# Top k of attention scores on pairs: the threshold from two sorted lists instead of one

## The chip, the cores and the metric

The kernel runs on one core of a Trainium2 chip. The time is the device time of one execution, in microseconds (us). TensorE (PE) does the matrix products, VectorE (DVE) the top-k search, ScalarE (ACT) copies, exponentials and activations, GpSimd (POOL) the masking, and SyncE (SP) issues the DMAs. Each engine works off its own queue in the order in which the program gives it work, and engines wait for one another through semaphores.

## The reference: what is computed

Attention that keeps only the 32 largest scores of each row, and behind it a two-layer perceptron:

```python
q, k, v: (8 batches, 8 heads, 576 positions, 64)  float32
scores = q @ k.T / sqrt(64)                       # 576 scores in a row
kth    = 32nd largest score of each row
scores = where(scores >= kth, scores, -1e9)
attn   = softmax(scores)
x      = (attn @ v), heads side by side           # (4608, 512)
h      = x @ w_in                                 # w_in  (512, 2048), float64
out    = max(0.01 * h, h) @ w_out                 # w_out (2048, 512), float64
```

A row's threshold `kth` is all that the top-k search has to deliver, with the row's maximum, which the softmax subtracts.

## The kernel before

**Units.** Heads are taken in pairs (32 pairs over the batches). A `Unit` is 128 query rows of both heads of a pair, or the 64 left-over rows of both heads of two pairs: 256 rows of scores in either case, held as two halves i = 0 and 1 of 128 partitions each. There are 144 units. A unit's scores lie in `u.both`, 128 partitions by 2 halves by 576 float32; `u.s[i]` is one half.

**One unit's way through the engines.** `scores` (L168): PE multiplies into PSUM, ACT copies to `s_sb` (L184). `top_k` (L186): DVE alone. It works in four rounds. In a round, an eight-largest instruction (`nc.vector.max`, MAX8 in the trace, L193) takes the eight largest of a half's 576 scores, for each half; then, in all rounds but the last, `match_replace` (MATCH_VALUE_LOAD and MATCH_REPLACE8 in the trace, L196) writes a copy in which these eight are overwritten by the lowest float. So each half has 4 MAX8 and 3 replacements, all 576 long; the 32nd largest is the last value of the fourth round. `mask` (L201): POOL computes `nbias` from the maximum (L205), then for each half `pen` = (score < threshold) * a large negative number (L207) and adds it to the scores (L209). `exponents`, `sums` and `normalize` run on ACT; `reciprocals` (L219) is one small DVE instruction in between (L221). `transpose` (L226) splits the floats into 16-bit halves on ACT (L233) and turns them with DMAs; `weigh_values` (L250) multiplies by v on PE. The perceptron (`mlp`, L269) works on chunks of up to 256 tokens on PE and ACT.

**The order of the work.** The schedule is written out by hand: a loop over steps (L392), one unit per step entering `top_k`, with the earlier units at later stages. In step s the top-k search is on unit s (`cur`), the mask on unit s-1 (`old`), the exponentials, the reciprocal, the normalization and the transposition on unit s-2 (`older`). `top_k` is a generator; each call of `slot(n)` (n = 0 to 3) runs it to its next `yield`, that is one round. Between the slots the loop puts perceptron matmuls (`mlp_steps`) on PE, by a budget that spreads the work at hand over the steps. The reciprocal stands behind `slot(2)`, so on DVE it lies in front of the last round. The scores of the next units are made ahead (`s_sb` has five buffers). Before the first unit, the weights are converted from float64 bits to float32 (`convert_weights`, L100 to L124), mostly on DVE.

The functions that the diff touches, with the line numbers of the profile:

Of the kernel before, what the change touches and what calls it, by code (L numbers as in the profile page):

```python
# [7 lines left out]
F32 = mybir.dt.float32  # L8
U32 = mybir.dt.uint32
U16 = mybir.dt.uint16  # L10
AF = mybir.ActivationFunctionType
ALU = mybir.AluOpType

NKC = 5

# [2 lines left out]
def kernel(  # L18
# [13 lines left out]
    nc = tc.nc  # L32
    NPAIR, P, S = qT.shape
    D = P // 2
    DFF, DMODEL = moe_w_out.shape[0], moe_w_in.shape[0]
    TOPK = 32
    SLOPE = 0.01
    LOWEST = -3.4028234663852886e38
    SCALE = float(D) ** -0.5
    MASKED = -1e9 / SCALE  # L40
    HP = DMODEL // P
    B = NPAIR // HP
    HS = S // 2
    NFC = DFF // P
    ROUNDS = TOPK // 8
    WCH = 1024
    LEFT = S % P
    assert D == 64 and S == 576 and HP == 4 and B % 2 == 0 and LEFT == 64
# [5 lines left out]
    const = ctx.enter_context(tc.tile_pool(name="const", bufs=1))  # L54
# [3 lines left out]
    work = ctx.enter_context(tc.tile_pool(name="work", bufs=2))  # L58
    small = ctx.enter_context(tc.tile_pool(name="small", bufs=5))
# [6 lines left out]
    range_lo, range_hi = ends[:, 0:1], ends[:, 1:2]  # L66
    nc.vector.memset(range_lo, -896.0)
    nc.vector.memset(range_hi, 255.0)

    w_in = [const.tile([P, DFF], F32, name=f"w_in{c}") for c in range(HP)]  # L70
    w_out = [const.tile([P, 4, DMODEL], F32, name=f"w_out{c}") for c in range(NFC // 4)]
# [28 lines left out]
    def convert_weights(dst, raw, on_vector):  # L100
# [6 lines left out]
        exf = ex.bitcast(F32)  # L107
        nc.vector.tensor_scalar(ex, hi, 20, 0x7FF, ALU.logical_shift_right, ALU.bitwise_and)  # L108
        nc.vector.tensor_scalar(man, hi, 0xFFFFF, None, ALU.bitwise_and)

        if on_vector:
            nc.vector.tensor_scalar(ex, ex, 1151.0, 896.0, ALU.min, ALU.max)
            nc.scalar.activation(ex, ex, AF.Copy, bias=-896.0 * 2.0 ** 23, scale=2.0 ** 23)
        else:
# [5 lines left out]
        nc.vector.scalar_tensor_tensor(out=dst, in0=man, scalar=2.0 ** -20, in1=frac,  # L120
                                       op0=ALU.mult, op1=ALU.add)
        nc.vector.scalar_tensor_tensor(out=ex, in0=hi, scalar=0x80000000, in1=ex,  # L122
                                       op0=ALU.bitwise_and, op1=ALU.bitwise_or)
        nc.vector.tensor_tensor(dst, dst, exf, ALU.mult)  # L124

# [59 lines left out]

    def top_k(u):  # L186

        u.tops = small.tile([P, 2, ROUNDS, 8], F32, name="tops")
        rest = [work.tile([P, S], F32, name=f"rest{i}", bufs=1) for i in range(2)]
        src = u.s  # L190
        for r in range(ROUNDS):
            for i in range(2):
                nc.vector.max(out=u.tops[:, i, r, :], in_=src[i])  # L193
            if r + 1 < ROUNDS:
                for i in range(2):
                    nc.vector.match_replace(out=rest[i], in_to_replace=u.tops[:, i, r, :],  # L196
                                            in_values=src[i], imm_value=LOWEST)
                src = rest
            yield

    def mask(u, i):  # L201
        if i == 0:
            u.nbias = small.tile([P, 2], F32, name="nbias")
            u.z = small.tile([P, 2], F32, name="z")
            nc.gpsimd.tensor_scalar(u.nbias, u.tops[:, :, 0, 0], -SCALE, None, ALU.mult)  # L205
        pen = work.tile([P, S], F32, name="pen", bufs=1)
        nc.gpsimd.tensor_scalar(pen, u.s[i], u.tops[:, i, ROUNDS - 1, 7:8], MASKED,  # L207
                                ALU.is_lt, ALU.mult)
        nc.gpsimd.tensor_tensor(u.s[i], u.s[i], pen, ALU.add)  # L209

    def exponents(u, i):
# [30 lines left out]
    def x_at(token):  # L242

        c = 0
        while token >= CHUNKS[c]:
            token -= CHUNKS[c]
            c += 1
        return c, token
# [89 lines left out]
    for n, u in enumerate(steps):  # L338
        if u is None:
            continue  # L340
        ch, _ = x_at(u.b * S + u.q0)
# [39 lines left out]
    with tc.manual_schedule():  # L381
# [10 lines left out]
        for s in range(len(steps) + LAG + 1):  # L392
            cur, old = unit(s), unit(s - 1)
            older, oldest, new = unit(s - 2), unit(s - LAG), ()
            if s % 2 == 0:
                new = [u for u in steps[s + 2:s + 4] if u]
            picks = top_k(cur) if cur else iter(())
            budget = slot_budget(s)

# [6 lines left out]
            if old:  # L406
                mask(old, 0)
                mask(old, 1)
# [91 lines left out]
```

## Time and profile before

| | |
|---|---|
| median of 3 runs | 1600.31 us (1598.17 to 1601.62) |
| profiled execution: time / span | 1596.01 us / 1594.1 us |
| mean granted TensorE clock | 0.988 |
| busy PE | 1396.0 us (88%) |
| busy DVE | 1480.3 us (93%) |
| busy ACT | 1115.8 us (70%) |
| busy POOL | 1078.6 us (68%) |
| DVE MAX8 (L193) | 608.2 us for 864 and 202.1 us for 288 instructions |
| DVE replacement (L196) | 423.6 us for 576 and 211.8 us for 288 instructions |
| POOL `pen` (L207) / add (L209) | 638.4 us / 406.5 us, 288 instructions each |

The profile is of one execution; its span is what lies between the first and the last instruction in it, its time some 2 us more. "Busy" is the time in which an engine had an instruction in it. Neighbouring instructions of DVE overlap by their ends: the mean length of one is longer than the distance from its start to the next one's start.

### The profile page before, as it was taken

How to read it: one execution, taken by the hardware profiler on the slowest of the kernel's cores; microseconds unless marked ns; L12 is line 12 of the kernel's file. 1: busy time of each engine (PE TensorE's matmuls, PEld its weight loads, DVE VectorE, ACT ScalarE, POOL GpSimd, SP SyncE). 2: the span in 40 equal slices, each digit the busy share in tenths (PEclk: the TensorE clock that was granted, in tenths of full speed). 3: DMA queues.
4: the chain of work that ended last, by engine and by line, in shares of the span. 5: the costliest groups of instructions: out<-in, count | busy, mean ns of one | idle time of the engine just before them, and what ended most of it. 6: DMA issues, size and time to landing. Idle time of an engine off the chain costs nothing.

```text
span 1594.1 us, 23761 instructions
## 1 busy us (share of the span) xinstructions
PE 1396.0 (88%) x8064; PEld 931.4 (58%) x8064; DVE 1480.3 (93%) x3114; ACT 1115.8 (70%) x2133; POOL 1078.6 (68%) x724
## 2 busy tenths in 40 slices
PE   0024977999999999999999999999999999999998
PEld 0013654757575757575757575757575756666664
DVE  8999989999999999999999999999999999999700
ACT  5626766778787877677877777777777777777720
POOL 0037767777777777777777777777777777777700
PEclk9998989999999999999999999999999999999999
DMA  6714436554655446544655456645655455545420
GB/s 226 268 42 119 120 112 184 146 147 126 185 142 149 133 127 184 161 114 131 192 142 144 132 133 173 169 127 136 184 150 148 121 161 135 157 121 141 128 68 14
DMA packets 400313, 227.00 MB, mean 142 GB/s; under 512 B 343360, under 2 KB 343360, under 8 KB 399168
## 3 DMA queue, kind: packets, MB, share of 16 engines
q1 hardware_dynamic: 400192, 225.49, 49.7%
q8 instruction: 63, 1.03, 0.3%
q14 instruction: 58, 0.48, 0.1%
HBM read 46.14 MB, written 94.37 MB: 88 GB/s over the span
## 4 chain that ended last, share of the span: by engine, by line
DVE 67%; PE 22%; ACT 6%; DMA 4%; issue 1%; SPq 0%; ACTq 0%
DVE tops L193 34%; DVE rest L196 28%; PE ph L277 10%; PE pz L289 6%; PE psc L175 3%; PE po L257 3%; ACT split L233 2%; DMA wT<-apart 2%; ACT s_sb L224 1%; DVE ex L122 1%; ACT s_sb L212 1%; DVE w_in L124 1%; DVE ex L108 1%; DVE w_in L120 1%; DMA apart<-split 1%
## 5 line engine op out<-in xcount | busy, mean ns | idle before, releaser
L207 POOL TENSOR_SCALAR pen<-s_sb,tops 128x576 f32<-128x576 f32 x288 | 638.4, 2216 | 304.6 <-DVE tops L193 272.2
L193 DVE MAX8 tops<-rest 128x8 f32<-128x576 f32 x864 | 608.2, 746 | 0.0
L277 PE MATMUL ph<-x,w_in 128*128 128x256 f32 (+1 forms) x2432 | 526.1, 373 | 40.7 <-ACT gT L283 40.7
L277 PEld LDWEIGHTS ph<-x,w_in 128*128 128x128 f32 x2432 | 440.1, 192 | 132.5 <-ACT gT L283 57.8
L289 PE MATMUL pz<-w_out,gT 128*128 128x512 f32 x1152 | 509.1, 597 | 3.4 <-ACT gT L283 3.4
L196 DVE MATCH_REPLACE8 rest<-tops,rest 128x576 f32<-128x576 f32 x576 | 423.6, 743 | 0.0
L209 POOL TENSOR_TENSOR s_sb<-s_sb,pen 128x576 f32<-128x576 f32 x288 | 406.5, 1412 | 24.0
L289 PEld LDWEIGHTS pz<-w_out,gT 128*128 128x128 f32 x1152 | 216.6, 191 | 269.2 <-issue 263.4
L224 ACT ACTIVATE s_sb<-s_sb,rz 128x576 f32<-128x576 f32 x288 | 207.3, 767 | 225.1 <-DVE rz L221 223.5
L233 ACT COPY split<-s_sb 128x1152 uint16<-128x1152 uint16 x288 | 318.0, 1154 | 2.3
L175 PE MATMUL psc<-kt,qt 64*128 64x288 f32 (+1 forms) x1280 | 201.2, 448 | 109.3 <-ACT s_sb L184 79.8
L212 ACT ACTIVATE s_sb<-s_sb,nbias 128x576 f32<-128x576 f32 x288 | 220.7, 773 | 15.4 <-POOL s_sb L209 15.4
L257 PE MATMUL po<-wT,vt 128*64 128x128 f32 (+1 forms) x3200 | 184.8, 270 | 40.1 <-DMA wT<-apart 38.8
L175 PEld LDWEIGHTS psc<-kt,qt 64*128 64x128 f32 (+1 forms) x1280 | 112.1, 185 | 180.7 <-ACT s_sb L184 86.6
L196 DVE MATCH_REPLACE8 rest<-tops,s_sb 128x576 f32<-128x576 f32 x288 | 211.8, 743 | 0.0
L257 PEld LDWEIGHTS po<-wT,vt 128*64 128x64 f32 x3200 | 162.7, 140 | 74.9 <-issue 40.1
L193 DVE MAX8 tops<-s_sb 128x8 f32<-128x576 f32 x288 | 202.1, 744 | 0.0
L283 ACT ACTIVATE gT<-ph 128x256 f32<-128x256 f32 (+1 forms) x304 | 109.5, 373 | 126.9 <-PE ph L277 124.7
L184 ACT COPY s_sb<-psc 128x576 f32<-128x576 f32 x288 | 169.9, 646 | 19.5 <-PE psc L175 19.2
L205 POOL TENSOR_SCALAR nbias<-tops 128x2 f32<-128x2 f32 x144 | 33.5, 233 | 105.2 <-DVE tops L193 92.4
L212 ACT ACTIVATION_READ_ACCUMULATOR s_sb<-s_sb,nbias 128x1 f32 x288 | 56.3, 195 | 0.0
L221 DVE RECIPROCAL rz<-ze 128x2 f32<-128x2 f32 x144 | 22.7, 157 | 30.6 <-ACT ze L217 30.4
(26 smaller groups left out, 292.9 us busy)
## 6 DMA issues: line engine op xcount, KB each, us to landing
apart<-split SPq DMA_DIRECT2D x288, 288.0 KB, 2.1
vt<-in_vk_dram SPq DMA_DIRECT2D x32, 320.0 KB, 3.4
qt<-in_qT_dram SPq DMA_DIRECT2D x32, 288.0 KB, 3.9
kt<-in_kT_dram SPq DMA_DIRECT2D x32, 288.0 KB, 4.5
out_dram<-o_sb SPq DMA_DIRECT2D x36, 256.0 KB, 2.6
raw<-in_moe_w_in_dram SPq DMA_DIRECT2D x8, 1024.0 KB, 5.1
raw<-in_moe_w_out_dram SPq DMA_DIRECT2D x8, 1024.0 KB, 4.9
wT<-apart SPq DMA_TRANSPOSE x144, 4.5
```

The source lines that it names most:

```text
L175: nc.tensor.matmul(ps[i][r0:r0 + u.rows, half, 0:HS], qt[d, u.q0:u.q0 + u.rows], kt[d, half * HS:(half + 1) * HS], start=True, stop=True,)
L184: nc.scalar.copy(u.s[i].rearrange("p (h n) -> p h n", h=2), ps[i][:, :, 0:HS])
L193: nc.vector.max(out=u.tops[:, i, r, :], in_=src[i])
L196: nc.vector.match_replace(out=rest[i], in_to_replace=u.tops[:, i, r, :], in_values=src[i], imm_value=LOWEST)
L207: nc.gpsimd.tensor_scalar(pen, u.s[i], u.tops[:, i, ROUNDS - 1, 7:8], MASKED, ALU.is_lt, ALU.mult)
L209: nc.gpsimd.tensor_tensor(u.s[i], u.s[i], pen, ALU.add)
L212: nc.scalar.activation(u.s[i], u.s[i], AF.Exp, bias=u.nbias[:, i:i + 1], scale=SCALE, accum_out=u.z[:, i:i + 1])
L224: nc.scalar.activation(u.s[i], u.s[i], AF.Copy, bias=0.0, scale=u.rz[:, i:i + 1])
L233: nc.scalar.copy(split, pairs[:, :, h])
L257: nc.tensor.matmul(po[side * D:(side + 1) * D, o, :], vt[:, c, side, :], u.wT[:, c + side * NKC if c + 1 < NKC else c, r:r + n], start=(c ...
L277: nc.tensor.matmul(ph[:, 0:n], w_in[c][:, f * P:(f + 1) * P], x[c][:, 0:n], start=(c == 0), stop=(c == HP - 1),)
L289: nc.tensor.matmul(pz[0:m, 0:DMODEL], gT[f][:, r0:r0 + m], w_out[f // 4][:, f % 4, :], start=(f == 0), stop=(f == NFC - 1),)
```

## The change

`top_k` no longer works on the 576 scores of a half, but on 288 pairs: score n of the first 288 with score n of the last 288. Two elementwise instructions over both halves (128 x 2 x 288) make `greater` (the larger of each pair) and `less` (the smaller). The search then takes the 16 largest of `less` (2 rounds) and the 32 largest of `greater` (4 rounds), each on 288 elements per half, with the replacement done in place. Of the 32 largest of all, at most 16 can be smaller ones of their pair, since the larger one stands before each. The 32nd of all is then the largest, over j = 0 to 16, of the lesser of two values: the j-th of the `less` list (plus infinity's stand-in for j = 0, kept in column 7 of the constant tile `lesser`) and the (32 - j)-th of the `greater` list. That is one elementwise minimum on 2 x 17 elements (`bounds`) and one reduction by maximum (`kth`).

The work per unit goes to the slots in another way: slot 0 now has the two elementwise instructions, the whole search of `less` and the first round of `greater`; slots 1 and 2 have a round of `greater` each, and slot 3 the last one, `bounds` and `kth`. The mask reads `u.kth` in place of the last value of the list.

```diff
+AX = mybir.AxisListType
...
-    ROUNDS = TOPK // 8
...
+    lesser = const.tile([P, 2, 8 + TOPK // 2], F32, name="lesser")
+    nc.vector.memset(lesser[:, :, 7:8], -LOWEST)
...
     def top_k(u):
 
-        u.tops = small.tile([P, 2, ROUNDS, 8], F32, name="tops")
-        rest = [work.tile([P, S], F32, name=f"rest{i}", bufs=1) for i in range(2)]
-        src = u.s
-        for r in range(ROUNDS):
-            for i in range(2):
-                nc.vector.max(out=u.tops[:, i, r, :], in_=src[i])
-            if r + 1 < ROUNDS:
+        u.tops = small.tile([P, 2, TOPK], F32, name="tops")
+        u.kth = small.tile([P, 2], F32, name="kth")
+        pairs = [work.tile([P, 2, HS], F32, name=name, bufs=1) for name in ("greater", "less")]
+        for of, op in zip(pairs, (ALU.max, ALU.min)):
+            nc.vector.tensor_tensor(of, u.both[:, :, 0:HS], u.both[:, :, HS:S], op)
+
+        def largest(of, n, to):
+            for r in range(n):
                 for i in range(2):
-                    nc.vector.match_replace(out=rest[i], in_to_replace=u.tops[:, i, r, :],
-                                            in_values=src[i], imm_value=LOWEST)
-                src = rest
-            yield
+                    nc.vector.max(out=to[:, i, 8 * r:8 * r + 8], in_=of[:, i, :])
+                if r + 1 < n:
+                    for i in range(2):
+                        nc.vector.match_replace(
+                            out=of[:, i, :], in_to_replace=to[:, i, 8 * r:8 * r + 8],
+                            in_values=of[:, i, :], imm_value=LOWEST)
+                    yield
+
+        for _ in largest(pairs[1], TOPK // 16, lesser[:, :, 8:]):
+            pass
+        yield from largest(pairs[0], TOPK // 8, u.tops)
+
+        bounds = small.tile([P, 2, TOPK // 2 + 1], F32, name="bounds", bufs=1)
+        nc.vector.tensor_tensor(bounds, u.tops[:, :, TOPK - 1:TOPK // 2 - 2:-1],
+                                lesser[:, :, 7:], ALU.min)
+        nc.vector.tensor_reduce(out=u.kth, in_=bounds, axis=AX.X, op=ALU.max)
+        yield
...
-            nc.gpsimd.tensor_scalar(u.nbias, u.tops[:, :, 0, 0], -SCALE, None, ALU.mult)
+            nc.gpsimd.tensor_scalar(u.nbias, u.tops[:, :, 0], -SCALE, None, ALU.mult)
...
-        nc.gpsimd.tensor_scalar(pen, u.s[i], u.tops[:, i, ROUNDS - 1, 7:8], MASKED,
-                                ALU.is_lt, ALU.mult)
+        nc.gpsimd.tensor_scalar(pen, u.s[i], u.kth[:, i:i + 1], MASKED, ALU.is_lt, ALU.mult)
```

Queue by queue, the other engines' instructions are the same in number and order; only what `pen` waits for is another instruction of DVE.

## The prediction

> **What bounds the kernel now.** First the page's busy shares, its slices and the chain that ended last.
>
> ```profile
> PE 1396.0 (88%) x8064; PEld 931.4 (58%) x8064; DVE 1480.3 (93%) x3114; ACT 1115.8 (70%) x2133; POOL 1078.6 (68%) x724
> ...
> DVE  8999989999999999999999999999999999999700
> ...
> DVE 67%; PE 22%; ACT 6%; DMA 4%; issue 1%; SPq 0%; ACTq 0%
> ```
>
> VectorE is full from the first slices to slice 38 (about 1506 us), and it carries two thirds of the chain. What follows is a tail of some 88 us of transposition and perceptron that the change doesn't touch. PE looks full too, but the busy table by stretches of 100 us has DVE at 100% in most of them, so DVE sets the pace. The question is the length of one unit on DVE. The timeline of DVE shows it (start, length, both in us):
>
> ```profile
> 801.57 1.41 DVE L193 MAX8 tops<-s_sb 128x8 f32<-128x576 f32 x2
> 802.89 0.08 DVE L196 MATCH_VALUE_LOAD rest<-tops,s_sb 128x8 f32 x1
> 802.95 0.75 DVE L196 MATCH_REPLACE8 rest<-tops,s_sb 128x576 f32<-128x576 f32 x1
> 803.61 0.09 DVE L196 MATCH_VALUE_LOAD rest<-tops,s_sb 128x8 f32 x1
> 803.68 0.75 DVE L196 MATCH_REPLACE8 rest<-tops,s_sb 128x576 f32<-128x576 f32 x1
> 804.34 1.42 DVE L193 MAX8 tops<-rest 128x8 f32<-128x576 f32 x2
> ...
> 809.88 0.16 DVE L221 RECIPROCAL rz<-ze 128x2 f32<-128x2 f32 x1
> 809.96 1.40 DVE L193 MAX8 tops<-rest 128x8 f32<-128x576 f32 x2
> 811.27 1.41 DVE L193 MAX8 tops<-s_sb 128x8 f32<-128x576 f32 x2
> ```
>
> The starts count, not the lengths, since neighbours overlap: an instruction lasts 0.746 but the next starts 0.66 later. A unit takes 811.27 - 801.57 = 9.70: four pairs of MAX8 (1.32, 1.33, 1.33, 1.31 from start to next start), three pairs of replacements (804.34 - 802.89 = 1.45) and the reciprocal (0.08). 144 units are 1397 us of the span. The waits of DVE in that stretch are small:
>
> ```profile
> DVE rz L221 <- ACT ze L217: 30.4, 14, 10.6
> ```
>
> 4.2 and 10.6 of these 30.4 us lie in the tail, 15.6 us among the units.
>
> Two more views price what is new. The timeline of the weight conversion has two-input elementwise instructions, and a dependence on the instruction directly before:
>
> ```profile
> 15.25 1.22 DVE L120 SCALAR_TENSOR_TENSOR w_in<-w_in,raw 128x1024 f32<-128x1024 uint32 x1
> 16.39 1.22 DVE L122 SCALAR_TENSOR_TENSOR ex<-raw,ex 128x1024 uint32<-128x1024 uint32 x1
> 17.64 1.23 DVE L124 TENSOR_TENSOR w_in<-w_in,ex 128x1024 f32<-128x1024 f32 x1
> ```
>
> L122 doesn't need L120's result and starts 1.14 after it; L124 needs L122's and starts 1.25 after it. So waiting for one's direct predecessor costs 0.11. Lastly, POOL's timeline in the same unit:
>
> ```profile
> 810.89 2.22 POOL L207 TENSOR_SCALAR pen<-s_sb,tops 128x576 f32<-128x576 f32 x1 [1.85 <-DVE tops L193]
> 813.20 1.42 POOL L209 TENSOR_TENSOR s_sb<-s_sb,pen 128x576 f32<-128x576 f32 x1
> 814.71 2.21 POOL L207 TENSOR_SCALAR pen<-s_sb,tops 128x576 f32<-128x576 f32 x1
> 817.01 1.41 POOL L209 TENSOR_TENSOR s_sb<-s_sb,pen 128x576 f32<-128x576 f32 x1
> 818.51 0.23 POOL L205 TENSOR_SCALAR nbias<-tops 128x2 f32<-128x2 f32 x1
> 820.59 2.22 POOL L207 TENSOR_SCALAR pen<-s_sb,tops 128x576 f32<-128x576 f32 x1 [1.85 <-DVE tops L193]
> ```
>
> `pen` starts 0.18 after the MAX8 that it waits for has ended (809.96 + 0.75 = 810.71). POOL works 7.85 of the 9.70 and is idle for 1.85.
>
> **The change on DVE, without other engines.** Fixed part and elements first, from start to start: MATCH_VALUE_LOAD takes 0.065 for 8 elements, MAX8 0.66 for 576, L120's form 1.14 for 1024. The slopes are (0.66 - 0.065) / 568 = 1.05 ns per element and (1.14 - 0.66) / 448 = 1.07. I take 1.05: an instruction of 288 is 0.30 shorter than one of 576, and the fixed parts are 0.055 for MAX8 and 0.065 for the two-input form. Removed per unit: 8 MAX8 and 6 replacements at 576. Added:
> - 6 pairs of MAX8 at 1.32 - 0.60 = 0.72: 4.34 (with the same spread of a hundredth by position).
> - 4 pairs of replacements at 1.45 - 0.60 = 0.85: 3.39.
> - `greater` and `less`, 576 elements each: 0.605 + 0.065 = 0.67, twice: 1.34. The first MAX8 on `less` needs the instruction directly before it: 0.11.
> - The last MAX8 is the direct predecessor of `bounds`: 0.11. `bounds`, 34 elements: 0.035 + 0.065, and `kth` waits for it: 0.11, together 0.21. `kth` to the next instruction: 0.10 (bounds: the reciprocal's 0.08 below, 0.2 above if reducing two short rows has a longer start; I take the value near the reciprocal's row, which is as small).
> - The reciprocal stays: 0.08.
>
> Sum: 4.34 + 3.39 + 1.34 + 0.11 + 0.11 + 0.21 + 0.10 + 0.08 = 9.68 against 9.70. The searched elements fall from 14 x 576 to 20 x 288, 2304 fewer or 2.4 us; six more fixed parts (0.06 for each of 4 MAX8, 0.12 with the value load for each of 2 replacements: 0.5), two passes over the data (1.34) and three waits (0.33) and the ending (0.2) eat all of it. By this sum alone the kernel gains 0.02 per unit, 144 x 0.02 = 3 us. An error of 0.1 per unit in the unmeasured parts would be 14 us either way.
>
> **What is moved.** POOL's `pen` now waits for `kth`, behind both last MAX8 and the two endings, not for the first of the two last MAX8; that is some 0.8 later in a unit, but it is later in each unit alike, so it costs that once, in the tail. The exponentials that follow run a step later (ACT waited for POOL's result 15.4 us in all, in two places). Behind the new waits on DVE only the top-k itself is queued. The reciprocal stands 0.8 from the unit's end as a MAX8 pair, `bounds` and `kth`, against 1.31 before: about half a microsecond later for ACT's normalization, which waited for it 223.5 us in all without being the bound, and as much more slack for `ze`. No DMA and no PE instruction moves.
>
> **What it collides with.** MAX8 and replacements read one tensor and keep 0.746 and 0.743 whatever POOL does beside them. `greater` and `less` read two, and no row of before has such an instruction beside a busy POOL: in the conversion POOL is idle. They come at a bad place. `kth` ends about 0.09 after `greater` has started, so by the 0.18 above `pen` starts some 0.27 after the start of `greater`, in all 143 units that follow another. Bounds for the cost on DVE: nothing (POOL waits, within its 1.85 of idle time), or one whole `pen`, 2.2, if `less` is held until `pen` ends. Nothing below zero: POOL gives DVE no time. Between them: both share reads element by element. A `pen` has a start of about 0.2 (the 2-element `nbias` takes 0.23), then 576 reads in 2.0, 3.5 ns each. From 0.47 to the end of `less` (1.35, less the tail gaps) some 0.75 us of reading overlaps: 214 reads, each in the time of one DVE element, 1.05 ns, are 0.22. I take 0.22, the value that needs no engine to win outright: 143 x 0.22 = 31 us.
>
> The Trainium skill, page "SBUF — State Buffer", section "Who interferes with whom", speaks against the change: a VectorE instruction with two SBUF inputs contends with a GpSimd instruction that reads SBUF, and the second to issue is blocked until the first has finished. By that rule the sum would lie at rival 1 if `pen` counts as issued before `less`, and at rival 2 if `less` is already queued; no row of before shows the case.
>
> **Forecast.** 1596.0 - 3 + 31 = 1624 against the profiled execution; the runs' median is 4.3 above that execution, which makes 1628, and I put 1626. Chance 0.38. Its own range is 1608 to 1650: 0.1 to 0.35 per unit and the rounding of the tie.
>
> **Rival 1, one `pen` per unit.** `less` starts when `pen` ends: `pen` gets its reads when `greater` has done its own (about 0.63 in) and ends 2.0 to 2.2 later, so `less` starts at 2.6 to 2.85 instead of 0.67, 1.95 to 2.2 late. Times 143: 279 to 315; DVE's own 15.6 us of waits may vanish beneath it. 1593 + 264 to 315 gives 1857 to 1908, likeliest 1885. For it: the fixed meeting of the two. Against: two queued DVE instructions leave a gap of 0.06 only. Chance 0.25.
>
> **Rival 2, no collision: a tie, or faster.** DVE keeps both instructions in front of `pen`; POOL loses about 1.1 of its 1.85 idle and still ends 0.1 to 0.4 before the next `bounds`. Then only DVE's sum decides, at 9.68 against 9.70: 1593, range 1576 to 1614. The place of the sign is the three waits for a predecessor, 0.33 per unit: if a short instruction's wait is cheaper than the 0.11 measured at 1024 elements, say 0.05, the gain is 0.18 x 144 = 26 us; from 0.11 on there is none, and a dearer `kth` turns it into a loss. Gains above 15 us or so would also be met by PE's places, where DVE waits for `ze` behind perceptron work. Chance 0.37, of which faster by over 0.2% 0.20, within 0.08, slower 0.09.
>
> **How the numbers follow.** A measurement of this kernel tells 0.2% (3.2 us) from no change. Slower: 0.38 + 0.25 + 0.09 = 0.72; same 0.08; faster 0.20. The forecast and rival 2 are near to each other in chance; the forecast leads by a little, since it needs no engine to win the whole meeting. The range leaves out the lower half of rival 2's gains and the upper third of rival 1: 1586 to 1896.
>
> **What would show it.** In the profile after: MAX8 at about 0.45 long and 0.36 apart, replacements alike; `greater` and `less` at 0.75 long if nothing collides, longer by 0.1 to 0.4 together in the forecast, or `less` near 2.9 long (or as late) in rival 1; `kth` waiting 0.11; `pen` longer than 2.22, or starting later. A unit of 9.9 is the forecast, 11.7 rival 1, 9.7 rival 2. The prediction is wrong altogether if the instructions at 288 are not 0.30 shorter, or if the reciprocal's waits for `ze` grow beyond 30 us.

## The result, and the profile after

The changed kernel takes 1607.57 us (median of 4 runs, 1607.22 to 1610.1) against 1599.72 us (4 runs, 1598.17 to 1601.62): slower, ratio 1.0052 with the interval 1.0035 to 1.0069. The two profiled executions lie further apart, 1607.56 against 1596.01, since the profiled execution of before was faster than each of these four runs. In the later comparisons the kernel before had medians of 1594 to 1595.

The page after, busy shares and the chain by engine:

```profile
PE 1400.9 (87%) x8064; PEld 934.7 (58%) x8064; DVE 1469.0 (91%) x4843; ACT 1115.4 (69%) x2133; POOL 1207.8 (75%) x724
...
DVE 66%; PE 21%; ACT 6%; DMA 5%; issue 2%; SPq 0%; DVEq 0%; ACTq 0%
```

The bound is the same engine. DVE is busy for 11 us less in a span that is 12 us longer, so the loss is in distances between instructions, not in their lengths. POOL is busy for 129 us more with the same 724 instructions. The timeline of DVE over one unit (start, length in us):

```profile
802.92 0.15 DVE L241 RECIPROCAL rz<-ze 128x2 f32<-128x2 f32 x1
803.00 0.80 DVE L203 MAX8 tops<-greater 128x8 f32<-128x288 f32 x2
803.83 0.20 DVE L217 TENSOR_TENSOR bounds<-tops,lesser 128x34 f32<-128x34 f32 x1
804.13 0.19 DVE L219 TENSOR_REDUCE kth<-bounds 128x2 f32<-128x34 f32 x1
804.23 0.75 DVE L198 TENSOR_TENSOR greater<-s_sb 128x576 f32<-128x576 f32 x1
804.90 0.75 DVE L198 TENSOR_TENSOR less<-s_sb 128x576 f32<-128x576 f32 x1
805.68 0.82 DVE L203 MAX8 lesser<-less 128x8 f32<-128x288 f32 x2
...
814.02 0.75 DVE L198 TENSOR_TENSOR greater<-s_sb 128x576 f32<-128x576 f32 x1
```

A unit is 814.02 - 804.23 = 9.79 (the median of all is 9.79 too), against 9.70. Of the pieces that were priced, six are where the sum had them, to 0.02: MAX8 pairs of 0.72 to 0.74, replacements of 0.85, passes of 0.67, 0.78 - 0.67 = 0.11 for the wait of the first MAX8 on `less`, 0.83 - 0.72 = 0.11 for the wait of `bounds`, 0.10 from `kth` to the next. `bounds` to `kth` is 0.30, not 0.21. And the passes are 0.75 long, as if POOL weren't there. POOL's timeline in the same unit:

```profile
804.51 3.14 POOL L228 TENSOR_SCALAR pen<-s_sb,kth 128x576 f32<-128x576 f32 x1 [1.03 <-DVE kth L219]
807.73 1.41 POOL L229 TENSOR_TENSOR s_sb<-s_sb,pen 128x576 f32<-128x576 f32 x1
809.24 2.21 POOL L228 TENSOR_SCALAR pen<-s_sb,kth 128x576 f32<-128x576 f32 x1
...
814.29 3.14 POOL L228 TENSOR_SCALAR pen<-s_sb,kth 128x576 f32<-128x576 f32 x1 [1.04 <-DVE kth L219]
```

The first `pen` of a unit starts 0.28 after `greater`, as forecast, and takes 3.14 where the second takes 2.21: the meeting happens, and POOL pays all of it, 0.93 a unit, out of its idle time, which falls from 1.85 to 1.03.

Where do the 0.09 between `bounds` and `kth` come from? In the first five units the distance is 0.23, from the sixth on 0.30. The instructions at the line of `kth` show what is new there:

```profile
L219 DVE TENSOR_REDUCE kth<-bounds x144: 187/189/190, 101.0 to 1517.2; 128x2 f32<-128x34 f32 x144
L219 DVEq EVENT_SEMAPHORE  x139: 21/21/21, 149.6 to 1517.2; - x139
```

144 reductions, and 139 waits of their own on DVE's queue, the first of them in the sixth unit. `kth` has five buffers, so from the sixth unit on the reduction waits for `bounds` and for POOL, which must have read the buffer's earlier content. The second wait is an instruction of its own, in front of an engine that has just run empty.

One more thing stands out. In 2 of 144 units a wait for "issue" made `greater` start 0.28 late, together with `pen`, and there `less` is longer and `pen` shorter than in the others. DVE, then POOL:

```profile
378.16 0.19 DVE L219 TENSOR_REDUCE kth<-bounds 128x2 f32<-128x34 f32 x1
378.55 0.78 DVE L198 TENSOR_TENSOR greater<-s_sb 128x576 f32<-128x576 f32 x1 [0.20 <-issue]
379.25 1.21 DVE L198 TENSOR_TENSOR less<-s_sb 128x576 f32<-128x576 f32 x1
380.50 0.82 DVE L203 MAX8 lesser<-less 128x8 f32<-128x288 f32 x2
```

```profile
378.54 2.79 POOL L228 TENSOR_SCALAR pen<-s_sb,kth 128x576 f32<-128x576 f32 x1 [1.04 <-DVE kth L219]
```

So the collision can cost DVE something, 0.46 here, and whether it does seems to hang on a few tenths of a microsecond.

### The profile page after: what moved, and what is told of

It is laid out like the page before. It is cut to its first block, busy times and chain, and to the rows that moved or that the text cites. A ratio compares the mean times of both kernels' runs of the same rounds, so it can differ in the third digit from the quotient of the medians.

```text
span 1605.8 us, 25630 instructions
## 1 busy us (share of the span) xinstructions
PE 1400.9 (87%) x8064; PEld 934.7 (58%) x8064; DVE 1469.0 (91%) x4843; ACT 1115.4 (69%) x2133; POOL 1207.8 (75%) x724
## 3 DMA queue, kind: packets, MB, share of 16 engines
q8 instruction: 63, 1.03, 0.3%
## 4 chain that ended last, share of the span: by engine, by line
DVE 66%; PE 21%; ACT 6%; DMA 5%; issue 2%; SPq 0%; DVEq 0%; ACTq 0%
DVE tops L203 18%; DVE greater L206 16%; DVE lesser L203 10%; PE ph L297 10%; PE pz L309 6%; DVE less L206 5%; DVE less L198 4%; DVE greater L198 4%; DMA wT<-apart 3%; PE po L277 3%; PE psc L179 3%; ACT split L253 3%; ACT s_sb L244 1%; DVE bounds L217 1%; DVE kth L219 1%
## 5 line engine op out<-in xcount | busy, mean ns | idle before, releaser
L228 POOL TENSOR_SCALAR pen<-s_sb,kth 128x576 f32<-128x576 f32 x288 | 768.6, 2669 | 184.5 <-DVE kth L219 162.9
L203 DVE MAX8 tops<-greater 128x8 f32<-128x288 f32 x1152 | 464.4, 445 | 0.0
L206 DVE MATCH_REPLACE8 greater<-tops,greater 128x288 f32<-128x288 f32 x864 | 376.1, 443 | 0.0
L203 DVE MAX8 lesser<-less 128x8 f32<-128x288 f32 x576 | 235.0, 449 | 5.0
L206 DVE MATCH_REPLACE8 less<-lesser,less 128x288 f32<-128x288 f32 x288 | 125.3, 443 | 0.0
L198 DVE TENSOR_TENSOR less<-s_sb 128x576 f32<-128x576 f32 x144 | 109.1, 758 | 0.0
L198 DVE TENSOR_TENSOR greater<-s_sb 128x576 f32<-128x576 f32 x144 | 107.9, 749 | 0.4 <-issue 0.4
```

The costliest lines, as they stand in the source:

```text
L198: nc.vector.tensor_tensor(of, u.both[:, :, 0:HS], u.both[:, :, HS:S], op)
L203: nc.vector.max(out=to[:, i, 8 * r:8 * r + 8], in_=of[:, i, :])
L206: nc.vector.match_replace(out=of[:, i, :], in_to_replace=to[:, i, 8 * r:8 * r + 8], in_values=of[:, i, :], imm_value=LOWEST)
L228: nc.gpsimd.tensor_scalar(pen, u.s[i], u.kth[:, i:i + 1], MASKED, ALU.is_lt, ALU.mult)
```

## The experiments

My theory after the result: the slowdown is the second wait of `kth` (139 x 0.07 = 9.7 us), on top of a tie of the rest, and the collision costs DVE nothing because both passes are lined up before `pen` asks. The rivals: the 0.07 comes from POOL's reads beside `bounds`; and, on the collision, that DVE is always served first, or that the first to come keeps the reads for its whole instruction. All kernels compute the reference in full; some add work that is not used.

### Seven buffers for `kth`

```diff
-        u.kth = small.tile([P, 2], F32, name="kth")
+        u.kth = small.tile([P, 2], F32, name="kth", bufs=7)
```

> Only the number of buffers of the threshold tile is changed, 5 to 7. Theory: in the changed kernel the reduction that makes kth starts 0.23 us after bounds in the first five units and 0.30 us after it from the sixth on, because from there on it waits for two engines, its predecessor on VectorE and GpSimd (which has to have read the buffer's earlier content); that second wait costs 0.07 us of VectorE in each of 139 units. With seven buffers the wait for GpSimd is already met by that of an earlier instruction. Expected: bounds to kth 0.23 us in all units, a unit of 9.72 us instead of 9.79, 139 x 0.07 = 9.7 us less than 1607.6, so about 1598 us, no difference from before (ratio 0.998 to 1.001). Rival: the 0.07 us comes from GpSimd's reads beside the two-input bounds, or from the instruction itself: then 0.30 us and 1607 us stay.

Measured: 1596.59 us against 1595.41, ratio 1.0006 (0.9996 to 1.0016). The median unit is 9.72. DVE's timeline has the short distance everywhere:

```profile
802.27 0.20 DVE L217 TENSOR_TENSOR bounds<-tops,lesser 128x34 f32<-128x34 f32 x1
802.50 0.19 DVE L219 TENSOR_REDUCE kth<-bounds 128x2 f32<-128x34 f32 x1
802.61 0.75 DVE L198 TENSOR_TENSOR greater<-s_sb 128x576 f32<-128x576 f32 x1
```

With the second wait gone (`kth` has none on DVE's queue in this trace), so is the whole loss, while `pen` and its collision are as in the changed kernel (3.15 us). This settles the sign: without that wait the change is a tie.

### `less` in the middle of POOL's add

In short, with comments for the reader:

```diff
-        for of, op in zip(pairs, (ALU.max, ALU.min)):
-            nc.vector.tensor_tensor(of, u.both[:, :, 0:HS], u.both[:, :, HS:S], op)
+        pair(0, ALU.max)            # greater
+        top(pairs[0], 0, u.tops)    # MAX8 of both halves
+        drop(pairs[0], 0, u.tops)   # replacement in both
+        top(pairs[0], 1, u.tops)
+        pair(1, ALU.min)            # less
...
```

> The pass that makes less is moved from directly behind greater into the middle of the search of greater, some 3.1 us after greater's start, where GpSimd is 0.2 us into its two-input add (1.41 us long). Its price is read from the length of less, 0.75 us in the changed kernel. Theory 1, the first to come has the reads until it has read all (as two odd units of the changed kernel show, where pen began with greater and less took 1.21 us, 0.46 longer, while pen ran 1.6 us beyond less's delayed start): the add reads 1152 elements, twice a pen's 576, so it has them for about 0.9 us and less waits some 0.7 us: length 1.4 to 1.5 us, a unit of 10.5 us, 1710 us in all. Theory 2, the first to come has the reads for its whole instruction: less waits 1.2 us, length 1.95 us, a unit of 11.1 us, 1790 us. Theory 3, VectorE is always served first: 0.75 us, the add longer by 0.6 us, a unit of 9.86 us (9.79, and one more instruction with two waits), 1618 us.

Measured: 1752.76 us, ratio 1.0984 (1.0964 to 1.1005); the median unit is 10.89. DVE around `less`, then POOL:

```profile
802.93 1.77 DVE L198 TENSOR_TENSOR less<-s_sb 128x576 f32<-128x576 f32 x1
804.63 0.08 DVE L206 MATCH_VALUE_LOAD greater<-tops,greater 128x8 f32 x1
```

```profile
802.69 1.40 POOL L241 TENSOR_TENSOR s_sb<-s_sb,pen 128x576 f32<-128x576 f32 x1
804.19 2.59 POOL L240 TENSOR_SCALAR pen<-s_sb,kth 128x576 f32<-128x576 f32 x1
```

`less` waits 1.02, more than theory 1's 0.7, less than theory 2's 1.2: the next start is 1.70 after its own instead of 0.67, so it got going at about 803.96, 0.13 before the add's recorded end at 804.09. Theory 3 falls: DVE isn't always served first. One more instruction got a second wait here, 139 times, the first MAX8 of `greater`, which now stands directly behind it: in the first five units it starts 0.78 to 0.79 after `greater`, from the sixth on 0.85 (799.77 to 800.62 in this unit). That is 0.07 again, and with it the unit is 9.79 + 0.07 + 1.02 = 10.88. Against before, 143 x 1.19 = 170 us of longer units, less 13 us of waits for `ze` that vanish (17.8 instead of 30.4), are the 157 us. The two theories that are left differ little for an add, whose reads may well last to its end; the `pen` is the better test.

### The two passes added to the kernel before

```diff
+        pairs = [rest[i].rearrange("p (i n) -> p i n", i=2) for i in range(2)]
+        for of, op in zip(pairs, (ALU.max, ALU.min)):
+            nc.vector.tensor_tensor(of, u.both[:, :, 0:HS], u.both[:, :, HS:S], op)
         src = u.s
```

> The kernel before with the two passes over the scores (greater and less) added and not used: the search stays as it was, 576 elements. They price the passes alone, and pen starts 0.38 us ahead of greater here, not 0.27 behind its start. The passes themselves add 1.34 us to a unit of 9.70: 11.04 us, 1600 + 193 = 1793 us, if VectorE is served first (theory 3: greater 0.75 us). Theory 1, the reads held for some 0.46 us out of a pen: greater waits 0.1 to 0.3 us, length 0.85 to 1.05 us, a unit of 11.25 us, 1820 us. Theory 2, held for the whole pen of 2.2 us: greater waits 1.8 us, length 2.6 us, a unit of 12.9 us, 2055 us.

Measured: 1805.06 us, ratio 1.1312 (1.1291 to 1.1333); the median unit is 11.27. DVE (the two passes are one line, x2), then POOL:

```profile
799.76 0.74 DVE L196 MAX8 tops<-rest 128x8 f32<-128x576 f32 x1
800.42 1.63 DVE L192 TENSOR_TENSOR rest<-s_sb 128x576 f32<-128x576 f32 x2
801.97 1.41 DVE L196 MAX8 tops<-s_sb 128x8 f32<-128x576 f32 x2
```

```profile
800.03 2.22 POOL L210 TENSOR_SCALAR pen<-s_sb,tops 128x576 f32<-128x576 f32 x1 [3.42 <-DVE tops L196]
```

The two passes take 801.97 - 800.42 = 1.55 instead of 1.34: one of them waited 0.21, although `pen` had started 0.39 before and ran on to 802.25. `pen` isn't lengthened. So a `pen` that comes first has the reads until some 0.6 after its start, not for its 2.2: theory 1, whose unit was 11.25. Two of the 143 units go another way:

```profile
766.75 3.51 POOL L210 TENSOR_SCALAR pen<-s_sb,tops 128x576 f32<-128x576 f32 x1 [3.70 <-DVE tops L196]
766.84 1.41 DVE L192 TENSOR_TENSOR rest<-s_sb 128x576 f32<-128x576 f32 x2
768.17 1.41 DVE L196 MAX8 tops<-s_sb 128x8 f32<-128x576 f32 x2
```

Here `pen` starts late, 0.10 before the passes, and waits for both, 1.29, while they take their 1.33. So a start that is recorded earlier by a tenth doesn't make `pen` the first to read. (The time lies below its 1820 us because the kernel before was at 1595 here and a slower DVE waits 14 us less for `ze`.)

### A fill between the passes

```diff
             nc.vector.tensor_tensor(of, u.both[:, :, 0:HS], u.both[:, :, HS:S], op)
+            if op == ALU.max:
+                nc.vector.memset(lesser[:, :, 6:7], 0.0)
```

> The changed kernel with one short instruction on VectorE, a fill of two elements, between greater and less. Theory: in the changed kernel pen asks for the reads while greater runs and still comes behind less, because less is already lined up behind greater; in the two odd units where greater started 0.28 us late, pen came in between and less took 1.21 us. A fill in between takes less out of the line: pen gets the reads when greater has done, for some 0.46 us, and less is 1.2 us long in all units; pen is 2.6 us long instead of 3.14; a unit of 9.79 + 0.06 + 0.46 = 10.3 us, 1607 + 74 = 1681 us. Rival: VectorE is served before GpSimd whenever it asks within a short gap, so the fill costs only itself: less 0.75 us, pen 3.2 us, a unit of 9.85 us, 1616 us.

Measured: 1606.66 us, ratio to before 1.0078 (1.0050 to 1.0105), the median unit 9.80. My theory's 1681 us was wrong, and the timeline of DVE says why:

```profile
803.47 0.75 DVE L198 TENSOR_TENSOR greater<-s_sb 128x576 f32<-128x576 f32 x1
804.15 0.75 DVE L198 TENSOR_TENSOR less<-s_sb 128x576 f32<-128x576 f32 x1
804.17 0.06 DVE L200 MEMSET lesser<- 128x2 f32 x1
```

The fill stands in front of `less` in the program but is recorded beside it, 0.02 after its start: it kept the passes 0.01 further apart and separated nothing. As a test of what lets `pen` in, this run decides nothing.

### `greater` 0.36 us later

```diff
+        spare = small.tile([P, 8], F32, name="spare", bufs=1)
+        nc.vector.max(out=spare, in_=u.both[:, 0, 0:HS])
         for of, op in zip(pairs, (ALU.max, ALU.min)):
```

> The changed kernel with one more MAX8 on 288 elements, its result unused, between kth and greater: the two passes come 0.36 us later against kth and so against pen, which then starts about 0.08 us before greater instead of 0.27 us after its start. (A fill between the passes, tried before this, ran beside less and separated nothing.) Theory, from the two odd units: asked for that early, the reads go to pen when greater has done, for some 0.46 us, before less is lined up: less 1.21 us, pen 2.7 to 2.8 us, a unit of 9.79 + 0.36 + 0.46 = 10.6 us, 1607 + 117 = 1724 us. Rival, two passes in a row are always served before GpSimd, and the odd units were late for another reason: less 0.75 us, pen 3.4 to 3.5 us, a unit of 10.15 us, 1659 us.

Measured: 1713.61 us, ratio 1.0742 (1.0695 to 1.0789); the median unit is 10.61. DVE, then POOL:

```profile
803.52 0.45 DVE L198 MAX8 spare<-s_sb 128x8 f32<-128x288 f32 x1
803.89 0.74 DVE L200 TENSOR_TENSOR greater<-s_sb 128x576 f32<-128x576 f32 x1
804.55 1.22 DVE L200 TENSOR_TENSOR less<-s_sb 128x576 f32<-128x576 f32 x1
805.80 0.82 DVE L205 MAX8 lesser<-less 128x8 f32<-128x288 f32 x2
```

```profile
803.80 2.84 POOL L230 TENSOR_SCALAR pen<-s_sb,kth 128x576 f32<-128x576 f32 x1 [2.15 <-DVE kth L221]
```

This is the odd unit, made regular: the median of `less` is 1.218, `pen` is 2.84. The added MAX8 costs 0.36 a unit, and the 0.36 by which it moves the passes towards `pen` costs another 0.47. The changed kernel escapes this price: there `greater` starts 0.28 before `pen`. In four units of this run `pen` starts at another distance. Twice it starts 0.20 after `greater`, and DVE pays nothing (`less` 0.75, `pen` 3.22); twice it starts earlier, 0.11 and 0.38 before `greater`, and `greater` itself waits (1.24 and 0.97 long) while `pen` takes 2.22. (The time is 10 us under the expected one; DVE waits 18.7 us for `ze` here, not 28.9.)

### The endings between the next unit's passes

In short, and in part in words:

```diff
+        ending = ended.pop() if ended else iter(())
         for of, op in zip(pairs, (ALU.max, ALU.min)):
             nc.vector.tensor_tensor(of, u.both[:, :, 0:HS], u.both[:, :, HS:S], op)
+            next(ending, None)      # bounds of the unit before; then its kth
...
-        bounds = ...                # bounds and kth at the unit's end
+        ended.append(threshold(u))  # the same two, made by next()
```

with `kth` in seven buffers and two pair buffers that swap roles from unit to unit.

> The next unit's two passes are put between the last searches and the ending of a unit (greater of the next unit, then bounds, then less of the next unit, then kth), with two pair buffers that change roles from unit to unit and with 7 buffers for kth. No instruction is then the direct successor of the one whose result it needs but for the first search of less, which has the short kth between. Theory: each such wait costs 0.11 us of VectorE, the second wait 0.07, and bounds and kth hide nothing else: a unit of 9.79 - 0.11 - 0.20 - 0.08 = 9.40 us, and 144 x 0.39 = 56 us less on VectorE than in the changed kernel. If VectorE alone sets the time: 1551 us. Rival: TensorE, 94 to 98% busy in the windows of before, becomes the bound and the reciprocals wait longer for ScalarE (30 us before): 1560 to 1590 us. Second rival, kth comes 1.3 us later and GpSimd, with 7.85 us of work in 9.40, still adds when the next greater begins: greater 0.1 to 0.9 us longer, and little or nothing is left of the gain (1570 to 1620 us).

Measured: 1581.83 us, ratio to before 0.9914 (0.9895 to 0.9932): faster than both kernels. DVE's timeline, then the chain and DVE's main wait:

```profile
799.57 0.74 DVE L202 TENSOR_TENSOR pair<-s_sb 128x576 f32<-128x576 f32 x1
800.22 0.19 DVE L228 TENSOR_TENSOR bounds<-tops,lesser 128x34 f32<-128x34 f32 x1
800.33 0.75 DVE L202 TENSOR_TENSOR pair<-s_sb 128x576 f32<-128x576 f32 x1
801.00 0.18 DVE L231 TENSOR_REDUCE kth<-bounds 128x2 f32<-128x34 f32 x1
801.11 0.82 DVE L208 MAX8 lesser<-pair 128x8 f32<-128x288 f32 x2
```

```profile
PE 63%; DVE 16%; ACT 13%; DMA 6%; issue 1%; SPq 0%; ACTq 0%
```

```profile
DVE rz L253 <- ACT ze L249: 59.0, 41, 10.4
```

The median unit is 9.36, 0.43 less than in the changed kernel (0.39 expected): with other work between, none of the waits shows. That is 62 us on DVE; 30 of them come back as waits of the reciprocal for `ze` (59.0 instead of 28.9), and the span is 28 us shorter. The chain passes from DVE (66%) to PE (63%), the first rival of this run. The passes stay at 0.75. POOL now starts its `pen` after both and meets them with `nbias` instead, which in 89 of the 144 units takes some 1.55 where it took 0.23, again out of POOL's idle time:

```profile
799.62 1.54 POOL L238 TENSOR_SCALAR nbias<-tops 128x2 f32<-128x2 f32 x1
```

### The search of `greater` first

```diff
-        for _ in largest(pairs[1], TOPK // 16, lesser[:, :, 8:]):
-            pass
-        yield from largest(pairs[0], TOPK // 8, u.tops)
+        of_greater = largest(pairs[0], TOPK // 8, u.tops)
+        next(of_greater)            # its first round
+        for _ in largest(pairs[1], TOPK // 16, lesser[:, :, 8:]):
+            pass
+        yield
+        yield from of_greater
```

with `kth` in seven buffers.

> Seven buffers for kth, and the first round on greater is put ahead of the search of less, so that no search follows directly on the pass that it needs. Theory: one wait for a direct predecessor, 0.11 us, is gone from the 9.72 us of the kernel with seven buffers: a unit of 9.61 us, 16 us less on VectorE. TensorE, on the longest chain with 63% in the kernel with the endings between the passes, takes part of it back: 1583 to 1592 us, ratio to before 0.992 to 0.998. Rival: that first search of greater now waits for two engines, and if that costs 0.07 us here as it did for kth, a unit is 9.68 us and the time 1591 to 1596 us; the theory says it is hidden, since VectorE is still at less when the wait is taken up.

Measured: 1585.89 us, ratio to before 0.9944 (0.9923 to 0.9964); the median unit is 9.59, 0.12 under the kernel with seven buffers (9.594 against 9.717). DVE's timeline, and the second waits at the line of the MAX8:

```profile
799.32 0.75 DVE L198 TENSOR_TENSOR greater<-s_sb 128x576 f32<-128x576 f32 x1
799.99 0.75 DVE L198 TENSOR_TENSOR less<-s_sb 128x576 f32<-128x576 f32 x1
800.66 0.81 DVE L203 MAX8 tops<-greater 128x8 f32<-128x288 f32 x2
```

```profile
L203 DVEq EVENT_SEMAPHORE  x139: 21/21/21, 140.1 to 1489.1; - x139
```

The MAX8 starts 0.67 after `less` in every unit, though it has a second wait as `kth` had. In these runs a second wait cost 0.07 behind the instruction whose result was needed (`kth`, and the MAX8 in the run with `less` in the add) and nothing here, where DVE was still at `less`.

## Why the prediction was right or wrong

**What bounds the kernel, and the sum on DVE: right.** Where POOL costs DVE nothing and the second wait is gone, the change is a tie: 9.68 against 9.70 in the sum, 9.72 measured with seven buffers. Each instruction of 288 elements is 0.30 shorter, as taken, and the three waits for a direct predecessor cost what the one in the weight conversion had shown: removing one gave 0.12 (9.717 to 9.594), removing all three 0.35 (9.717 to 9.363), 0.12 each.

**The direction: right by luck, through a cost that isn't in the sum.** Slower was forecast for the collision, which cost DVE nothing. The term that was missing is in the line for `bounds` and `kth`: 0.21 was put down for the distance between them, and it is 0.30. 0.07 of it is the second wait, 139 times, 9.7 us, and with seven buffers the time is that of before. Rival 2 had named the place ("a dearer `kth` turns it into a loss"), but neither the reason nor the price. The section on moved steps asked who waits for `kth`, not whom `kth` waits for: a new tile with five buffers that POOL reads brings a wait of DVE for POOL with it, which can be read off the program without a run; its price can't.

**The collision: the term that was mis-sized.** 0.22 per unit, 31 us, was taken on the ground that both engines would share the reads element by element; it measured nothing on DVE (`greater` 0.749, `less` 0.758 on average, with two odd units in that). Sharing element by element is not what the runs show. One side reads and the other waits: POOL waits 0.93 in the changed kernel while the passes keep their length, DVE 0.21, 0.47 or 1.02 in the experiments, depending on the order in which they come. So rival 2 described the meeting correctly ("DVE keeps both instructions in front of `pen`"), POOL's idle time covered the 0.93 as it said, and the time came out on the slower side of its range. The argument against rival 1, that two queued DVE instructions leave too short a gap, isn't what decided: with `greater` 0.36 later the passes stand as close (0.66 from start to start), and `pen` gets in between. Then the price is 0.47, not the 2.0 of rival 1.

**The page that spoke against the change.** The Trainium skill, "SBUF — State Buffer", section "Who interferes with whom", was right that such a VectorE instruction and a GpSimd instruction block each other rather than share, and that the order decides, though a recorded start 0.10 earlier did not make `pen` the first in two units. That the second is blocked until the first has finished, as the same page's section "Summary: rules for kernel authors" has it, is not what these runs show for `pen`: `less` waited 0.47 for a `pen` of 2.84 and ended long before it. For the two-input add it is nearly so, 1.02 of the 1.16 that were left of it.

**PE as the next bound: right as far as the chain shows.** It was named only as a limit to gains "above 15 us or so". The kernel that gains 62 us on DVE has PE on 63% of its chain and keeps 28.

## What to carry to other kernels

Count, for each new buffer that another engine reads, the wait that its reuse brings to the writer, and see whether the writer already waits for something there: two buffers more made 10 us of 1600 here. Splitting a long instruction into shorter ones pays its fixed part and puts results next to their use; work that is independent, put in between, took back three waits of 0.12 a unit. Before costing a collision of two engines by a rate, find out which of them comes first, and by how much: a small margin is a risk, here 0.47 a unit.

## What was not expected of the hardware

- A second semaphore wait in front of a DVE instruction is recorded as an instruction of its own on DVE's queue (21 ns) and delayed the start by 0.07 us where DVE had run empty (0.23 to 0.30 at `kth`, 0.78 to 0.85 at a MAX8); where DVE was still at work it delayed nothing (0.67 from `less` to the next MAX8).
- A one-input `pen` on POOL, 2.2 us long, keeps a two-input DVE instruction waiting for some 0.46 us, not for its length: its reads seem to be over about 0.6 after its start. The two-input add kept it waiting up to 0.13 before the add's end.
- Two two-input DVE instructions in a row held POOL off through both (`pen` 3.14 instead of 2.21) when `pen` started 0.28 after the first, but let it in between when `pen` started 0.09 before the first. A sharp border in the recorded starts there is not: in two units of the kernel with the added passes `pen` started 0.10 before the first and waited for both (3.51). What decides between the two, a line of requests or the moment at which the second is taken up, stays open: the run that was to tell it, with the fill, separated nothing.
